# A new written order for the first five groups of an attention and two-layer kernel, with the first transposes in PSUM banks of their own

## The chip, the cores and the metric

The kernel runs on one core of a Trainium2 chip. The metric is the device time of one execution in microseconds (us), the median over repeated runs. Engines are named as the profile names them: PE (TensorE matmul) and PEld (its weight loads), DVE (VectorE), ACT (ScalarE), POOL (GpSimd), SP (SyncE, which here only issues transfers).

## The reference

```python
# attention: 4 sequences, 8 heads, 768 positions, 64 per head
scores = scale * q @ k.T                       # per sequence and head
keep   = (pos_k < 8) | ((0 <= rel) & (rel < 96))   # 8 global keys, 96 local ones
dist   = where(global and not local, 96, abs(rel))
scores = where(keep, scores - slope[h] * dist, -1e9)
a      = softmax(scores);  attn = a @ v
# two layers on the 3072 tokens of 512
x = attn.transpose(0, 2, 1, 3).reshape(3072, 512)
h = x @ w_in                                   # 512 -> 2048
g = max(h, 0) + log1p(exp(-abs(h)))            # softplus
out = g @ w_out                                # 2048 -> 512, float32
```

## The kernel before

The 3072 tokens are 24 blocks of 128. Two neighbouring blocks of one sequence are a unit (12 of them), and two blocks are a group of 256 tokens for the two layers (12 groups). A block needs the keys of itself, of the block before it, and the 8 global keys of its sequence, which are copied over unused rows of the block before.

Every piece of work is an operation with a name, made by `op(name, engine, ...)`. The string `ORDER` lists all 1046 names in one sequence, each with the engine that runs it (P = PE, V = DVE, A = ACT, G = POOL, S = SP); the program is issued in exactly that sequence, so each engine has its own fixed queue, in the order of the string. An engine that waits holds up all that is behind it in its queue. The names:

- `ldq3`, `ldk3`, `ldv3` load unit 3; `win0` to `win7` and `wout0` to `wout7` load the 512 KB pieces of the weights, all through SP (the first q also through ACT). `castq`, `castk`, `castv`, `cin`, `cout` turn them into bf16.
- `trq`, `trk` transpose q and k: for units 0 to 2 on PE, into PSUM, with `cpq`, `cpk` copying them out; from unit 3 on by DMA transposes that SP issues.
- `sb` writes the bias into PSUM by a matmul (blocks 0 and 1), `sc6.0` are the scores of block 6 (two parts for some blocks), `z` adds the bias on DVE, `ex` is the exponential on ACT, `pv` the product with v, `nm` the normalisation on DVE, `xt`, `xc` the transpose of the block's result into XT (a DMA transpose from block 6 on). `gk`, `gv` copy global keys and values.
- `a5.3` is piece 3 of 8 of the first layer of group 5: 8 matmuls of 128x256 into one of two PSUM banks, h0 and h1 by turns; `e5.3` is its exponential on ACT, which frees the bank, and `ln5.1` the logarithm for two pieces.
- Groups 0 and 1 take the second layer plainly: `b0.1.4` are two matmuls of 128x512 of group 0, token block 1, from row piece 4 on; `oc` copies the sum out of PSUM. From group 2 on the 2x2 block product is made of seven products, `b2.3` and so on, of sums of weights (`ws`, made once) and of tokens (`ka`), with `oe` gathering them out of PSUM. `st` stores.
- `fill0` to `fill34` are matmuls on a blank tile that nothing reads. They write the bank x.

PSUM has eight banks: two tiles s0 and s1 of two banks each, h0, h1, x and o. Unit 0's transposes are made in two halves (`SPLIT`): both halves of q go to the two banks of tile s0 and both halves of k to those of s1. Accesses are ordered by a key for the whole tile (`held` cuts a key to its tile), so that the second half's score work waits for both halves' copies.

The operations that the prediction speaks of: the fillers (line 1235), unit 0's transposes (790) and their copies (793), later transposes on PE (810) and copies (817), score matmuls (950; block 0's are 887 and 897, block 1's bias is 931), first-layer matmuls (1060), plain second-layer matmuls (1107), weight casts (643), casts of q, k, v (658, 674, 686, 706), first-layer exponentials (1075).

## Time and profile before

| what | value |
|---|---|
| median of 3 runs | 210.25 us (210.16 to 210.38) |
| span of the profiled execution, first to last instruction | 208.3 us |
| mean granted TensorE clock | 0.997 |
| busy in the span | PE 97%, ACT 81%, DVE 77%, POOL 54% |
| moved by DMA | 40.99 MB, mean 197 GB/s |

The profiled execution's span leaves out what lies ahead of its first and behind its last instruction, so it is 1.95 us below the median of the runs. Rows of the profile give start and length, engine, line, operation, output<-input; `x8` is the number of instructions that a row merges. `[0.66 <-ACT ident_q]` is idle time in front of it and what ended it. The end of a matmul is modelled, and neighbouring matmuls overlap in such rows. Times are from the span's start.

### The profile page before, as it was taken

The page shows a single profiled execution, that of the slowest core. Times are in us where ns is not written, and L with a number is a line of the kernel's source. Part 1 is how long each engine was busy: PE and PEld are TensorE (multiplying, and loading weights), DVE is VectorE, ACT ScalarE, POOL GpSimd, SP SyncE. Part 2 cuts the span into 40 slices and gives each one's busy share as a digit, 9 for nine tenths or more (in the row PEclk, how much of TensorE's full clock was granted, in tenths as well). Part 3 has the DMA queues.
Part 4 walks back from the last instruction along what each step waited for, and adds up shares of the span by engine and source line. Part 5 has one row for each costly group of instructions (what it writes and reads, how often), then busy time and mean ns, then how long its engine had stood idle before and what let it go on. Part 6 is the DMA issues. An engine that isn't in the chain of part 4 may idle for free.

```text
span 208.3 us, 5515 instructions
## 1 busy us (share of the span) xinstructions
PE 201.5 (97%) x2211; PEld 164.8 (79%) x2211; DVE 159.8 (77%) x296; ACT 169.0 (81%) x240; POOL 112.8 (54%) x127
## 2 busy tenths in 40 slices
PE   7789999999999999999999999999999999999993
PEld 2455887756678889888888898888888889888882
DVE  5589899899888798786989995928897684434383
ACT  4698899998999987998879989679879895897300
POOL 4356262708686367742867699655707506623540
PEclk9999999999999999999999999999999999999998
DMA  5999999999998999679999979573742204200205
GB/s 175 364 361 388 387 358 361 332 245 249 201 271 214 257 210 312 172 188 296 195 212 259 191 200 221 145 152 102 106 73 62 92 5 142 63 0 0 104 22 181
DMA packets 70650, 40.99 MB, mean 197 GB/s; under 512 B 30433, under 2 KB 62689, under 8 KB 70625
## 3 DMA queue, kind: packets, MB, share of 16 engines
q1 hardware_dynamic: 69936, 39.99, 77.2%
q10 hardware_dynamic: 688, 0.66, 1.0%
q8 instruction: 17, 0.28, 0.5%
q14 instruction: 9, 0.07, 0.1%
HBM read 27.26 MB, written 6.29 MB: 161 GB/s over the span
## 4 chain that ended last, share of the span: by engine, by line
PE 85%; DMA 8%; DVE 2%; POOL 2%; issue 1%; ACTq 0%; ACT 0%; POOLq 0%; DVEq 0%
PE h_ps L1060 38%; PE o_ps L521 25%; PE s_ps L950 5%; PE x_ps L1002 4%; PE s_ps L1107 3%; DMA raw<-in_q_dram 3%; DMA kT<-kb 3%; DMA XT<-xs 2%; PE x_ps L1235 2%; PE x_ps L521 2%; PE s_ps L521 1%; PE s_ps L810 1%; POOL vb L706 1%; PE o_ps L1107 1%; PE o_ps L1002 1%
## 5 line engine op out<-in xcount | busy, mean ns | idle before, releaser
L1060 PE MATMUL h_ps<-XT,w_in_bf 128*128 128x256 bf16 x768 | 94.4, 273 | 0.1
L1060 PEld LDWEIGHTS <-w_in_bf 128*128 128x128 bf16 x768 | 73.2, 98 | 11.0 <-DMA XT<-xs 0.3
L1075 ACT ACTIVATE e<-h_ps 128x512 f32<-128x512 f32 x96 | 60.1, 637 | 17.6 <-PE h_ps L1060 16.6
L1086 ACT ACTIVATE g<-e 128x1024 bf16<-128x1024 f32 x48 | 49.8, 1053 | 0.6
L976 DVE TENSOR_TENSOR z<-s_ps,biasA 128x1024 f32<-128x1024 f32 x38 | 45.9, 1218 | 3.5 <-PE s_ps L950 3.1
L983 ACT ACTIVATE pb<-z 128x1024 bf16<-128x1024 f32 (+1 forms) x44 | 43.4, 993 | 1.3 <-DVE z L976 0.6
L451 POOL TENSOR_TENSOR g<-g 128x1024 bf16<-128x1024 bf16 x11 | 23.9, 2171 | 23.7 <-DVE raw L451 23.5
L521 PEld LDWEIGHTS <-g 128*128 128x128 bf16 x320 | 30.9, 98 | 3.6
L451 POOL TENSOR_TENSOR raw<-g 128x1024 bf16<-128x1024 bf16 x9 | 19.6, 2177 | 15.0 <-ACT g L1086 13.5
L868 POOL COPY vb<-vb 4x512 bf16<-4x512 bf16 x22 | 14.9, 675 | 20.9 <-PE x_ps L1002 16.2
L706 POOL CAST vb<-raw 64x512 bf16<-64x512 f32 x32 | 21.6, 678 | 6.0 <-DMA raw<-in_v_dram 4.7
L521 PEld LDWEIGHTS <-raw 128*128 128x128 bf16 x240 | 22.6, 98 | 2.8
L521 PE MATMUL o_ps<-raw,raw 128*128 128x256 bf16 x192 | 24.3, 273 | 0.0
L451 DVE TENSOR_TENSOR raw<-g 128x1024 bf16<-128x1024 bf16 x21 | 17.2, 829 | 6.5 <-ACT g L1086 4.1
L521 PE MATMUL o_ps<-raw,g 128*128 128x256 bf16 x160 | 19.6, 273 | 0.0
L1002 PEld LDWEIGHTS <-pb 128*128 128x128 bf16 x352 | 16.4, 98 | 3.6 <-ACT pb L983 0.6
L1014 DVE TENSOR_TENSOR xs<-x_ps,rcp 128x256 bf16<-128x256 f32 x40 | 17.0, 424 | 1.4
L1002 PE MATMUL x_ps<-vb,pb 128*128 128x65 bf16 x304 | 15.8, 193 | 0.0
L521 PE MATMUL o_ps<-w_out_bf,g 128*128 128x256 bf16 x128 | 15.8, 273 | 0.0
L1235 PE MATMUL x_ps<-blank 128*128 128x512 bf16 x35 | 11.7, 454 | 1.2 <-DVE blank L1159 1.2
L1013 DVE RECIPROCAL rcp<-x_ps 128x4 f32<-128x4 f32 x40 | 7.1, 178 | 7.4 <-PE x_ps L1002 6.8
L674 POOL CAST qb<-raw 128x1024 bf16<-128x1024 f32 (+1 forms) x9 | 9.3, 1032 | 5.9 <-DMA raw<-in_q_dram 5.6
(123 smaller groups left out, 216.3 us busy)
## 6 DMA issues: line engine op xcount, KB each, us to landing
raw<-in_v_dram SPq DMA_DIRECT2D x12, 512.0 KB, 5.7
out_dram<-osb SPq DMA_DIRECT2D x22, 256.0 KB, 2.5
raw<-in_q_dram SPq DMA_DIRECT2D x9, 512.0 KB, 4.9
raw<-in_k_dram SPq DMA_DIRECT2D x9, 512.0 KB, 5.5
raw<-in_moe_w_in_dram SPq DMA_DIRECT2D x8, 512.0 KB, 9.3
raw<-in_moe_w_out_dram SPq DMA_DIRECT2D x8, 512.0 KB, 9.1
raw<-in_k_dram SPq DMA_DIRECT2D x6, 256.0 KB, 5.9
raw<-in_q_dram SPq DMA_DIRECT2D x4, 256.0 KB, 7.0
```

Of the source, the lines that this page charges most:

```text
L451: (nc.vector if eng == "DVE" else nc.gpsimd).tensor_tensor(dst, a[0], b[0], ALU.subtract)
L521: nc.tensor.matmul(psum(j), lhs[:, f // 2, f % 2, :], w(f), start=(f == 0 and not (chain and j in "267")), stop=(f == 7), skip_group_check ...
L706: copy_on[eng](dst, src)
L868: copy_on[eng](vb_of(prev)[sl, :, 0:D], vb_of(first)[sl, :, 0:D])
L976: nc.vector.tensor_tensor(z, src, bias, ALU.add)
L983: nc.scalar.activation(pb[:, 0:nr, :].rearrange("p (y a) b -> p y (a b)", y=2), src, AF.Exp, scale=1.0 / root_d)
L1002: nc.tensor.matmul(xv[:, h, :], pb[:, 4 * (h % 2) + 2 * part + h // 2 if lone else u_all * (2 * (h % 2) + h // 2) + u, :], vb_of(prev if u ...
L1014: nc.vector.tensor_tensor(xs[:, 4 * part : 4 * part + 4, :], xv[:, :, 0:D], rcp[:][:, :, None].to_broadcast([P, 4, D]), ALU.mult,)
L1060: last = nc.tensor.matmul(hv[:, j, :], w_in_bf[:, m, fb * P : fb * P + P], XT[g % NXG][:, m, :], start=(m == 0), stop=(m == NM - 1),)
L1075: nc.scalar.activation(e[:, p % 2, :, :].rearrange("p j (b t r) -> p (j b) r t", b=2, r=2), hb[:].rearrange("p (a r t) -> p a r t", a=4, r=2),
L1086: nc.scalar.activation(gt[:, 2 * p - 2 : 2 * p + 2, :].rearrange("p a t -> p (a t)"), e[:].rearrange("p a j t -> p (a j t)"), AF.Ln, bias=1.0,
L1235: nc.tensor.matmul(x_ps[:], blank[:, 0:P], blank[:])
```

## The change

Four things change.

1. `ORDER` is written anew from the start to the fourth group's second-layer products on PE (`b3.4` is the first of a tail of 154 PE operations that is the same in both; the other engines' tails agree from about the same place). The set of operations is the same. 76 of them run on another engine.
2. Unit 0's transposes get a home each (`SPLIT_KEYS`): q's halves go to the first bank of s0 and to o, k's halves to the first bank of s1 and to x, and each is ordered by its own bank.
3. The fillers are made in two lots: 22 ahead of all loads, the others behind unit 0, ordered against all users of the bank x, since a transpose of k is now made there.
4. The copies of global keys and values are no longer held behind the exponential of the block before; what they read and write still orders them.

In `ORDER`, 19 fillers stand ahead of the first transposes `trq0.0` (12 before) and 16 behind it (23 before). On SP the first 27 transfers are the same; behind `wout5` the order changes up to the transfers of unit 7. On PE the scores of block 4 and the first half of block 5 (`sc4.0`, `sc5.0`) now stand ahead of the first-layer piece `a0.7`; before, `sc5.0` stood behind `b0.0.4`. A piece of the string, where `sc5.0` is now, and the rest of the diff:

```diff
-nm3.1:V cin6:G a0.4:P e0.5:A cpq2.0:V wout4:S xt3:P e0.4:A cin7:V sc4.0:P xc3:V ln0.2:A a0.7:P wout5:S z4.0:V cout0:G
+cin5:V pv3.0:P ex3.1:A sc4.0:P nm3.0:V cin4:G e0.3:A z4.1:V pv3.1:P fill34:P gk5:A a0.5:P e0.2:A cin6:G z4.0:V wout4:S
...
-FILLERS = 35
+FILLERS = 22, 35
...
+SPLIT_KEYS = {"q": (("s", 0, 0), ("o",)), "k": (("s", 1, 0), ("x",))}
...
         if i in SPLIT:
             for x in range(2):
-                tr = s_ps[key[1]][:, x, :].bitcast(BF16)[:, 0:512]
+                home = SPLIT_KEYS[which][x]
+                tr = bank(home).bitcast(BF16)[:, 0:512]
...
-                sub = [("sub", which, i)] if x else []
                 op(f"tr{which}{i}.{x}", "PE", 0.225, rank + 0.05 * x, mm, count=4,
-                   reads=[(which + "b", i % NQB, 2 * x + z) for z in range(2)] + ["ident_q"] + (held([key]) if x else []),
-                   writes=sub or held([key]))
+                   reads=[(which + "b", i % NQB, 2 * x + z) for z in range(2)] + ["ident_q"], writes=held([home]))
                 outs = [("qT", i % NQT, x)] if which == "q" else [kt_tile(i) + (x, r) for r in range(2)]
-                op(f"cp{which}{i}.{x}", engs[x % len(engs)], 0.0, rank + 0.1 * x, ev, reads=held([key]) + sub,
+                op(f"cp{which}{i}.{x}", engs[x % len(engs)], 0.0, rank + 0.1 * x, ev, reads=held([home]),
                    writes=outs, alts={"DVE": 0.36, "ACT": 0.51})
...
         op(f"gk{n}", "POOL", 0.25, rank, copies,
-           reads=kt_keys(first), writes=kt_keys(prev), after=since, port=True,
+           reads=kt_keys(first), writes=kt_keys(prev), port=True,
            alts={"POOL": 0.25, "DVE": 0.14, "ACT": 0.14})
...
-    def filler(j):
-
+    def fillers(js):
         def fn():
             nc.tensor.matmul(x_ps[:], blank[:, 0:P], blank[:])
-        return op(f"fill{j}", "PE", 0.216, 1e6 + j, fn, reads=["blank"],
-                  after=[pl.writer[("x",)]] if j else [])
+        for j in js:
+            last = op(f"fill{j}", "PE", 0.216, 1e6 + j, fn, reads=["blank"], after=users(("x",)))
+            pl.writer[("x",)], pl.readers[("x",)] = last, []
...
-    for j in range(FILLERS):
-        pl.writer[("x",)] = filler(j)
+    fillers(range(FILLERS[0]))
...
             attend_in(i, at_block(n0) - 6.0)
+            if not i:
+                fillers(range(*FILLERS))
```

Three places as the engines' queues show them. The first is POOL's queue where the later pieces of w_in are cast, before (cin2, castq2.0, gk8, gv8.1, cin6, and the casts of w_out):

```order
L643 CAST w_in_bf<-raw_76 128x2x512
L674 CAST qb_81<-raw_69 128x8x64
L852 COPY kTa_92<-kTa_92 128x4x8
L868 COPY vb<-vb 4x8x64
L643 CAST w_in_bf<-raw_67 128x2x512
L643 CAST w_out_bf<-raw_72 128x1024
```

and now (cin2, castq2.0, castk2.1, cin4, cin6, cin7, gk8, cout0):

```order
L644 CAST w_in_bf<-raw_76 128x2x512
L675 CAST qb_81<-raw_69 128x8x64
L675 CAST kb_83<-raw_68 128x8x64
L644 CAST w_in_bf<-raw_77 128x2x512
L644 CAST w_in_bf<-raw_67 128x2x512
L644 CAST w_in_bf<-raw_79 128x2x512
L852 COPY kTa_92<-kTa_92 128x4x8
L644 CAST w_out_bf<-raw_72 128x1024
```

Two pieces of w_in, raw_77 (cin4) and raw_79 (cin7), have come from DVE to POOL, and one half of k's cast with them.

The second is ACT's queue from the exponential e1.2 to the copies of group 0's output, before:

```order
L1075 ACTIVATE e_106<-h_ps_64 128x4x2x64
L1075 ACTIVATE e_106<-h_ps_65 128x4x2x64
L643 CAST w_out_bf<-raw_75 128x1024
L1086 ACTIVATE g_107<-e_104 128x1024
L1075 ACTIVATE e_104<-h_ps_65 128x4x2x64
L643 CAST w_out_bf<-raw_77 128x1024
L674 CAST qb_82<-raw_67 128x1024
L1075 ACTIVATE e_104<-h_ps_64 128x4x2x64
L1086 ACTIVATE g_108<-e_106 128x1024
L1038 COPY XT_120<-x_ps 128x4x128
```

and now:

```order
L644 CAST w_out_bf<-raw_75 128x1024
L1075 ACTIVATE e_106<-h_ps_64 128x4x2x64
L707 CAST vb<-raw_74 64x8x64
L1075 ACTIVATE e_106<-h_ps_65 128x4x2x64
L1086 ACTIVATE g_107<-e_104 128x1024
L1086 ACTIVATE g_108<-e_105 128x1024
...
L1086 ACTIVATE g_108<-e_106 128x1024
L1075 ACTIVATE e_104<-h_ps_65 128x4x2x64
L1075 ACTIVATE e_104<-h_ps_64 128x4x2x64
...
L687 CAST kb_84<-raw_68 128x1024
L983 ACTIVATE pb_100<-z_95 128x1024
```

The casts of v of unit 2 (raw_74, three of them) and of k of unit 3 (raw_68) have come to ACT; one cast of w_out (raw_77), the cast of q of unit 3 (raw_67) and the copy to XT have left it.

The third is SP's queue from the loads of unit 3 on, before:

```order
L608 DMA raw_67<-in_q_dram 128x8x128
L608 DMA raw_68<-in_k_dram 128x8x128
L639 DMA raw_79<-in_moe_w_out_dram 128x2x512
L639 DMA raw_78<-in_moe_w_out_dram 128x2x512
L608 DMA raw_69<-in_v_dram 128x8x128
L837 DMA_TRANSPOSE qT_85<-qb_82 128x8x128
L608 DMA raw_74<-in_q_dram 128x8x128
L830 DMA_TRANSPOSE kT_89<-kb_84 128x8x64
L608 DMA raw_75<-in_k_dram 128x8x128
```

and now:

```order
L640 DMA raw_78<-in_moe_w_out_dram 128x2x512
L609 DMA raw_69<-in_v_dram 128x8x128
L609 DMA raw_68<-in_k_dram 128x8x128
L609 DMA raw_67<-in_q_dram 128x8x128
L640 DMA raw_79<-in_moe_w_out_dram 128x2x512
L609 DMA raw_74<-in_q_dram 128x8x128
L830 DMA_TRANSPOSE kT_89<-kb_84 128x8x64
L837 DMA_TRANSPOSE qT_85<-qb_82 128x8x128
```

wout7 (raw_79) has moved behind v, k and q of unit 3, the load of q of unit 4 (raw_74) ahead of unit 3's transposes, and k's first transpose ahead of q's.

167 lines of the change are left out of this document (83 added, 84 removed).

## The prediction

> **What bounds the kernel now.** I read the page first, then busy times by stretch, then the filler matmuls, then the chain of waits. The page's first part and its slices:
>
> ```profile
> PE 201.5 (97%) x2211; PEld 164.8 (79%) x2211; DVE 159.8 (77%) x296; ACT 169.0 (81%) x240; POOL 112.8 (54%) x127
> PE   7789999999999999999999999999999999999993
> DMA  5999999999998999679999979573742204200205
> ```
>
> TensorE is busy from the third slice to the last; the DMA engines are full for the first dozen slices (5.2 us each). By stretches (length, then PE, PEld, DVE, ACT, POOL, and the granted clock, DMA share, GB/s):
>
> ```profile
> 6.70:16.00 9.30, 8.08 (x108) 5.25 (x107) 6.57 (x19) 7.94 (x14) 5.03 (x8) 1.00 1.08 366
> 16.00:28.40 12.40, 12.40 (x153) 9.39 (x147) 10.71 (x25) 10.85 (x17) 5.81 (x8) 1.00 1.05 387
> 28.40:50.00 21.60, 21.60 (x202) 14.66 (x199) 20.74 (x35) 20.69 (x28) 9.86 (x13) 1.00 1.14 308
> 50.00:66.00 16.00, 15.79 (x190) 11.82 (x188) 14.28 (x25) 14.98 (x21) 11.14 (x17) 1.00 1.17 220
> 66.00:90.00 24.00, 24.00 (x280) 20.96 (x277) 20.40 (x36) 21.32 (x30) 15.81 (x20) 1.00 1.05 235
> 90.00:200.00 110.00, 110.00 (x1241) 97.04 (x1240) 78.21 (x134) 89.62 (x124) 62.38 (x54) 1.00 0.59 132
> ```
>
> TensorE is idle for 1.22 us (9.30 - 8.08) between 6.7 and 16, and from there on only for 0.21 us between 50 and 66. Part of what it does is filler, though. The filler line alone, over the whole run and by stretch, and three rows of the timeline:
>
> ```profile
> L1235 PE MATMUL x_ps<-blank x35: 378/379/634, 1.2 to 25.6; 128*128 128x512 bf16 x35
> 6.70:12.50 5.80, 1.57 (x5) 0.40 (x5) 1.00 1.10 352
> 12.50:28.40 15.90, 5.22 (x18) 1.59 (x18) 1.00 1.05 387
> 28.40:208.00 179.60, 0.00 (x0) 0.00 (x0) 1.00 0.76 174
> 1.17 4.90 PE L1235 MATMUL x_ps<-blank 128*128 128x512 bf16 x12 [1.17 <-DVE blank L1159]
> 6.72 0.38 PE L790 MATMUL s_ps<-ident_q,qb 128*128 128x128 bf16 x4 [0.66 <-ACT ident_q L1170]
> 19.72 1.24 PE L1235 MATMUL x_ps<-blank 128*128 128x512 bf16 x5
> ```
>
> Five fillers take 1.24 us where one alone shows 0.38, so each occupies (1.24 - 0.38) / 4 = 0.216 us and a lone matmul shows some 0.16 us of tail that the next one overlaps. So TensorE's time is: 6.72 us before the first useful matmul, useful work that no order changes, 23 fillers of 0.216 = 4.97 us after that, and waits. From 28.4 us to the end no filler is left and hardly a wait: what the change does beyond there can only be lost, or gained in tenths. What the changed order can win lies ahead of 28.4 us, and all that counts is how much useful work TensorE has behind it there.
>
> **The early orders.** After the change 19 fillers stand ahead of the first transposes, not 12. Eleven of the twelve old ones start by 5.69 us (1.17 + 4.90 = 6.07 us is the end of the twelfth, less its 0.38 us); seven more and that twelfth put trq0.0 at 5.69 + 8 x 0.216 = 7.42 us, 0.70 us later than 6.72. Its inputs are earlier, so the fillers decide. Behind it 16 fillers stand where 23 stood: 7 x 0.216 = 1.51 us less. If no wait changed, the gain would be 1.51 - 0.70 = 0.81 us; the waits decide.
>
> The first loads keep their order, so they keep their arrival; these rows start when one lands:
>
> ```profile
> 5.65 0.62 ACT L658 CAST qb<-raw 128x512 bf16<-128x512 f32 x1 [0.45 <-DMA raw<-in_q_dram]
> 6.41 0.43 DVE L658 CAST kb<-raw 128x512 bf16<-128x512 f32 x1 [0.29 <-DMA raw<-in_k_dram]
> 7.32 0.61 POOL L658 CAST qb<-raw 128x512 bf16<-128x512 f32 x1 [2.42 <-DMA raw<-in_q_dram]
> 7.90 0.87 DVE L658 CAST kb<-raw 128x512 bf16<-128x512 f32 x1 [0.87 <-DMA raw<-in_k_dram]
> 10.53 1.09 ACT L910 ACTIVATE pb<-h_ps 128x512 bf16<-128x512 f32 x2 [0.77 <-PE h_ps L897]
> 15.75 0.41 PE L950 MATMUL s_ps<-qT,kTa 64*128 64x128 bf16 x8 [0.48 <-ACT kTa L817]
> ```
>
> The second q half is cast on VectorE (0.43 us, as the k row shows) from 7.3 to 7.75 and the second k half on GpSimd (0.61) from 7.9 to 8.5; if VectorE took 0.87 again, trq0.1 would still be ready at its turn. Transposes in banks of their own then follow each other without waiting for one another's evacuation: trq0.0 7.42, trk0.0 7.85, trq0.1 8.28, the bias seed 8.7, and block 0's scores at 9.2 us. The ScalarE row above, the first exponential, would start near 9.6 instead of 10.53. From there softmax, normalisation and the transposes of unit 1 chain through ScalarE and VectorE much as before, and sc2.0 comes at about 15.6 us against 15.75: the lead is spent again. Three rows of weights set the posts after that:
>
> ```profile
> 19.98 1.04 POOL L643 CAST w_in_bf<-raw 128x1024 bf16<-128x1024 f32 x1 [1.57 <-DMA raw<-in_moe_w_in_dram]
> 26.52 1.04 POOL L643 CAST w_in_bf<-raw 128x1024 bf16<-128x1024 f32 x1
> 27.39 0.71 DVE L643 CAST w_in_bf<-raw 128x1024 bf16<-128x1024 f32 x1 [0.37 <-DMA raw<-in_moe_w_in_dram]
> 28.43 1.92 PE L1060 MATMUL h_ps<-XT,w_in_bf 128*128 128x256 bf16 x16
> 17.71 0.40 PE L950 MATMUL s_ps<-qT,kTa 64*128 64x128 bf16 x8
> 18.05 0.39 PE L1235 MATMUL x_ps<-blank 128*128 128x512 bf16 x1
> ```
>
> The changed order wants a0.2 next after the first pieces, and its w_in piece (cin2) is cast at 19.98 + 1.04 = 21.02 us: a0.2 waits about 0.5 us for it. The last post is cin7: it lands at 27.39 as now, but its cast moves from VectorE (0.71) to GpSimd (1.04), so a0.7 can start at about 27.39 + 1.04 = 28.43, which is where it starts now. What has been done by then differs: sc4.0 runs three microseconds earlier, and half of block 5's scores, sc5.0, is already done. Eight score matmuls cost 18.05 - 17.71 = 0.34 us and another 0.1 us in front, where they follow wider matmuls. So **term one: -0.43 us**, from a post that the DMA sets. Below it the end is TensorE's own pace: with cin7 in time it would be there some 0.2 us sooner. Above it is zero, should a0.7 come 0.4 us late.
>
> **From 28.4 to 50 us.** Here TensorE, ScalarE (20.69 of 21.60) and VectorE (20.74) are all full, and the change gives ScalarE more work. Prices per piece, ScalarE between 28 and 48 us by groups, and two rows of the timeline, the second being sc6.0:
>
> ```profile
> L1075 ACT ACTIVATE e<-h_ps 128x512 f32<-128x512 f32 x11 | 7.0, 644 | 0.5 <-PE h_ps L1060 0.4
> L643 ACT CAST w_out_bf<-raw 128x1024 bf16<-128x1024 f32 x2 | 2.1, 1044 | 0.0
> L1136 ACT COPY osb<-s_ps 128x512 f32<-128x512 f32 x1 | 0.6, 586 | 0.5 <-PE s_ps L1107 0.5
> L852 ACT COPY kT<-kTa 128x32 bf16<-128x32 bf16 x1 | 0.2, 237 | 0.0
> 49.48 0.62 ACT L706 CAST vb<-raw 64x512 bf16<-64x512 f32 x1
> 49.06 0.62 PE L950 MATMUL s_ps<-qT,kT 64*128 64x128 bf16 x16
> ```
>
> To ScalarE come, between the first exponential and sc6.0: two w_in casts (1.04 each; the trace has only w_out's on ScalarE, the same size, and two casts of 0.62 would be 1.24), three v casts and two casts of q and k (0.62 each), one cast of a whole k (1.04), cpq2.0 and oc0.1.0 (0.59 each) and a short copy (0.24): 7.6 us. Away go two casts of 1.04, xc1, xc4, cpk2.1 and cpq1.1 (0.59 each), one v cast (0.62) and two short copies (0.48): 5.5 us. Net +2.1 us. Against that stand the earlier start (0.9) and ScalarE's idle time, 1.55 us in 16 to 28.4 (12.40 - 10.85) and 0.91 in the next stretch, 2.46 together. If all of it is used, ScalarE ends this stage 1.3 us earlier than now; if none is, 1.2 us later. I take it as just keeping up, since it idles for z tiles and matmuls that come earlier in the new order. Walking the rows, b0.1.14 falls near 46.6, oc0.0.0 ends near 48.5 and sc6.0 starts near 48.6, while now it starts at 49.06: the 0.43 of term one, kept. **Term two: 0**, between -0.5 (TensorE's own pace, if it got there sooner) and +1.6 (1.2 late, and term one lost).
>
> The transfers here: k of the fourth unit before q, and wout7 behind both. The queue is full, so wout7 comes two loads later (2 x 0.52 MB at 308 GB/s, 3.4 us); walking the queue, its cast ends near 46.3 against b0.1.14's turn at 46.6, and the transposes of the fourth unit land near 48.3 against sc6.0 at 48.6. Cover is 0.3 us for each; where it is gone, the stall is as long as the lateness.
>
> **From 50 us.** The 0.21 us of idle time are three pauses, and each hides a 0.16 us overlap as well: about 0.6 us in all. Rows of the timeline for the first and the chain of waits for the others:
>
> ```profile
> 52.41 0.42 PE L1002 MATMUL x_ps<-vb,pb 128*128 128x65 bf16 x8
> 52.39 5.58 DMA kT<-kb
> 58.02 0.62 PE s_ps L950 x16
> 60.56 4.29 DMA XT<-xs
> 64.90 1.92 PE h_ps L1060 x16
> ```
>
> At 52.41 pv6.0 waits for its exponential; the new order puts a third first-layer piece (0.87 us) in front of it. At 58.02 the scores of block 8 wait for the DMA transpose of k; the new order issues it ahead of ldv4 and ldq5, two loads of 1.7 us each at that rate, and the wait was 0.3 us. At 64.90 a3.1 waits for the transposed block 7, which queues behind trq5 now and ahead of it then. All three go: -0.6. I give 0.15 back for b1.1.0, whose bank is freed by oc1.0.0, moved from ScalarE to a full VectorE. **Term three: -0.45** (0 to -0.6). Beyond, both orders keep TensorE full, and from b3.4 on they are the same, so what is gained by then stays. Weight sums and token sums that move to GpSimd are the dearest pieces there:
>
> ```profile
> L451 POOL TENSOR_TENSOR g<-g 128x1024 bf16<-128x1024 bf16 x11 | 23.9, 2171 | 23.7 <-DVE raw L451 23.5
> ```
>
> Even at 2.17 us, ka2.2, the last of them before convergence that TensorE takes soon, ends a microsecond before b2.2 by my walk; if it did not, b2.2 would wait for what is missing.
>
> **Sum.** -0.43 + 0 - 0.45 = -0.88 us on a span of 208.3 us, 207.4. The runs stand at 210.25, 1.95 above the span; the same distance gives **209.4 us**.
>
> **The rivals.** *More is won*: the early chain keeps its lead of 0.9 us, the new waits are none. The most it can be: now 4.97 of fillers and some 2.5 of waits (1.22 with four overlaps of 0.16, and 0.6), then 0.70 + 16 x 0.216 = 4.16 and no wait: 3.3 us, 207.0. Against it: the weights' arrivals do not move. From 208.6 down to half of that, 0.14. *It cancels*: cin7 or a late evacuation eats term one and the DMA queue shifts its own stall; 209.83 to 210.67, chance 0.22. *Slower, by ScalarE*: its added work is not absorbed between 20 and 48 us, the banks of first-layer pieces come free late, and TensorE waits for e tiles between a1.1 and sc6.0. It decides from the point where ScalarE recovers less than 1.2 us (2.1 - 0.9) of its 2.46 us of idle time; with none, sc6.0 is 1.2 us late, less the 0.45 of term three: +0.75, 211.0. For it: ScalarE is at 96% (20.69 of 21.60) there, and three v casts stand in the middle of its new list. Against it: nine pieces leave it in the same stage. Chance 0.14. *Slower, by the clock*: seven fillers fewer let TensorE pause, and its clock drops. The twelve fillers of the 4.90 us row stand (4.90 - 0.38) / 11 = 0.41 us apart, not 0.216; such a spell again costs 11 x 0.19 = 2.1 us: 211.5. The longest pause in the trace after the start is 0.66 us and the clock column stays at 1.00; my longest new wait is 0.55. Chance 0.03. The Trainium skill's page "TensorE: Matmul & The Clock Gate", section "What's actually happening", has the clock halve after an idle window of about 3.4 us; by that rule nothing drops here, and the trace agrees, 0.66 us of pause with a clock of 1.00. *The orders don't do what they say* has no room: they are the program's own instruction order.
>
> **How the numbers follow.** The forecast, 208.6 to 209.83, has 0.47, more gained 0.14, cancelled 0.22, slower 0.17. A difference of 0.2%, 0.42 us, is about the least that a measurement of this kernel tells from none: faster 0.61, same 0.22, slower 0.17. The range is 208.3 to 210.9: it leaves out the larger part of the big gain and of the slow cases. The likeliest case's own range is 208.6 to 209.8.
>
> **What would show it.** Right: trq0.0 near 7.4; the first exponential near 9.6; a0.7 near 28.4 with sc5.0 ahead of it; sc6.0 near 48.6; no TensorE idle time at the places of 52.41, 58.02 and 64.90. Wrong: idle time of TensorE in front of first-layer pieces, released by ScalarE, between 30 and 48 us; sc6.0 released by a DMA; b0.1.14 behind the cast of wout7; a first-layer piece behind a w_in cast later than 28.9.

## The result, and the profile after

The changed kernel took 212.87 us (median; single values 212.19, 212.23, 213.51, 213.52) against 210.31 us of the kernel before beside it: ratio 1.0113, 95% interval 1.0078 to 1.0148. It is slower by 1.1%; the forecast was 209.4 us. Measured again on another chip it took 214.77 us (212.90 to 215.44) against 210.56: ratio 1.0179 (1.0142 to 1.0216). The profiled execution took 212.23 us with a span of 210.4 us, 2.1 us more than the 208.3 before; what follows looks at that execution first, and then at others.

The page of the changed kernel, its first part and two rows of its slices (forty equal slices of the span, the granted clock and the DMA engines' busy share in tenths):

```profile
PE 202.2 (96%) x2202; PEld 163.9 (78%) x2211; DVE 161.6 (77%) x300; ACT 171.8 (82%) x245; POOL 110.4 (52%) x118
PEclk9999999999999999999999999999999999999999
DMA  5999999998999999999999969675651302300205
```

Nine matmul records are missing (2202 of 2211), so idle time of TensorE is better read from starts than from busy sums. Its granted clock is full throughout. The waits of TensorE in that page's execution (who waited for what, sum, times, longest); none of the three reached 0.2 us in the kernel before:

```profile
PE h_ps L1060 <- DMA XT<-xs: 1.3, 2, 0.7
PE s_ps L950 <- DMA kT<-kb: 0.4, 1, 0.4
PE s_ps L950 <- DMA qT<-qb: 0.2, 1, 0.2
```

Four rows of the timeline of the changed kernel, TensorE, are its posts: a0.7 (merged with no other), sc6.0, sc13.0, and the last row of products; behind them the last two of these in the kernel before:

```profile
28.27 0.60 PE L1060 MATMUL h_ps<-XT,w_in_bf 128*128 128x256 bf16 x4
49.02 0.56 PE L950 MATMUL s_ps<-qT,kT 64*128 64x128 bf16 x14
91.30 0.40 PE L950 MATMUL s_ps<-qT,kTa 64*128 64x128 bf16 x8
206.25 0.82 PE L522 MATMUL h_ps<-raw,raw 128*128 128x256 bf16 x6
```

```profile
90.05 0.45 PE L950 MATMUL s_ps<-qT,kTa 64*128 64x128 bf16 x10
203.68 0.71 PE L521 MATMUL h_ps<-raw,raw 128*128 128x256 bf16 x5
```

The matmuls that stand ahead of sc6.0 are the same set in both orders, and so are those ahead of sc13.0; from sc13.0 on the sequence is the same too. So the differences of these starts are gains and losses, without any correction:

| start of | before | changed | difference |
|---|---|---|---|
| a0.7 (with sc5.0, 0.43 us, done only in the changed one) | 28.43 | 28.27 | -0.16, with sc5.0 -0.59 |
| sc6.0 | 49.06 | 49.02 | -0.04 |
| sc13.0 | 90.05 | 91.30 | +1.25 |
| last row of products | 203.68 | 206.25 | +2.57 |
| end of the span | 208.3 | 210.4 | +2.1 |

The early order won 0.59 us by 28 us and had lost it by 49. From sc6.0 to sc13.0 it lost 1.29 us, and 1.32 us more behind sc13.0, where both kernels run the same matmuls in the same sequence. (What lies behind the last products was 0.44 us shorter; nothing here was tried on that.) The places, in TensorE's timeline of the changed kernel (pv7.0, a3.1, sc10.0, sc14.0, a6.0; idle time in brackets):

```profile
58.75 0.40 PE L1002 MATMUL x_ps<-vb,pb 128*128 128x65 bf16 x8
65.76 0.50 PE L1060 MATMUL h_ps<-XT,w_in_bf 128*128 128x256 bf16 x3 [0.61 <-DMA XT<-xs]
73.33 0.57 PE L950 MATMUL s_ps<-qT,kT 64*128 64x128 bf16 x14 [0.17 <-DMA qT<-qb]
96.93 0.23 PE L950 MATMUL s_ps<-qT,kT 64*128 64x128 bf16 x2 [0.41 <-DMA kT<-kb]
109.45 0.61 PE L1060 MATMUL h_ps<-XT,w_in_bf 128*128 128x256 bf16 x4 [0.67 <-DMA XT<-xs]
```

Each idle time in brackets hides an overlap besides, because rows that follow each other without a wait overlap (a first-layer piece starts 0.16 us before the shown end of the row ahead, a score piece 0.07). With it the waits are: a3.1 0.78, sc10.0 0.24, sc14.0 0.48, a6.0 0.84. There are smaller ones at pv7.0 (0.30), at pv7.1 (0.28, for the normalisation nm7.0), at sc11.0 (0.15) and at sc8.0 (0.10). Together that is 3.2 us, where the kernel before has 0.5 at pv6.0, sc8.0 and a3.1. Up to sc13.0 the waits add up to 1.8 us against 0.5 before, and behind it to 1.3 against none: that is the whole of the two losses, +1.29 and +1.32.

Which transpose comes late is not the same in every execution. A second profiled execution of the same kernel (after_again below) waits 0.84 us at pv8.0, 0.83 at sc11.0, 0.60 at sc7.0 and 0.55 at a6.0, but 0.07 at a3.1 and not at all at sc14.0; from sc6.0 to its last products it takes 157.48 us against 157.23 here. So the sum hardly varies and the places do, and a single wait below 1 us in one trace is weak evidence for what an edit does.

**How a3.1 came to wait in this execution.** The chain of waits of the changed kernel from 58 to 66 us:

```profile
58.20 0.64 DVE vb L868
58.84 1.13 DVE z L976
60.09 0.42 DVE xs L1014
60.52 0.59 DVE kT L855 x2
61.23 0.42 DVE xs L1014
61.68 4.04 DMA XT<-xs
65.76 0.28 PE h_ps L1060
```

The transposed block 7 (xt7) is issued at 61.68 instead of 60.56, and takes 4.04 us. In front of it VectorE has no gap: two copies of global values (57.06 to 58.84), the bias sum z8.0, and only then the normalisations nm7.0 and nm7.1. In the kernel before nm7.0 stood ahead of z8.0 and one of the copies was on GpSimd. GpSimd meanwhile shows why pv7.0 was late (timeline, changed kernel: castk5.0, ws3.7, castv3.11):

```profile
55.74 1.04 POOL L687 CAST kb<-raw 128x1024 bf16<-128x1024 f32 x1 [1.26 <-ACT g L1086]
56.74 1.28 POOL L417 TENSOR_TENSOR raw<-raw 128x512 bf16<-128x512 f32 x1
58.08 0.61 POOL L707 CAST vb<-raw 64x512 bf16<-64x512 f32 x1
```

castv3.11 needs v of unit 3, there since 40.43, but stands behind a cast that waits for ldk5 (landed 55.59, whatever the row names) and behind a weight sum.

**How sc14.0 and a6.0 came to wait.** sc14.0 needs the transpose trk7.0, which in the new order of SyncE stands behind xt11, a store and the load ldq8, and stood ahead of all three before. Its row in SyncE's queue (issue time, how long SyncE was held), changed and before:

```profile
92.34 1.39 SPq L830 DMA_TRANSPOSE kT<-kb  x1
```

```profile
85.15 2.01 SPq L830 DMA_TRANSPOSE kT<-kb  x1
```

In the changed kernel it landed at 96.88, and sc14.0 started at 96.93. So SyncE's two orders agree only from the load ldv9 on (93.79 in the changed kernel) and GpSimd's only from castk8.0 on, later than TensorE's, which agree from b3.4. The place of trk7.0 was not changed by itself in any run; in gv7_on_gpsimd below it has the same place, landed at 95.68, and sc14.0 did not wait.

The next three transposes in SyncE's queue, changed and before (trk7.1, xt12, xt13):

```profile
97.04 3.91 SPq L830 DMA_TRANSPOSE kT<-kb  x1
101.05 1.21 SPq L1045 DMA_TRANSPOSE XT<-xs  x1
105.08 1.22 SPq L1045 DMA_TRANSPOSE XT<-xs  x1
```

```profile
94.35 3.36 SPq L830 DMA_TRANSPOSE kT<-kb  x1
97.81 1.37 SPq L1045 DMA_TRANSPOSE XT<-xs  x1
102.51 1.19 SPq L1045 DMA_TRANSPOSE XT<-xs  x1
```

SyncE runs 2.6 to 3.2 us behind, while TensorE at sc13.0 is 1.25 us behind: the queue is later than the work that waits for it. For xt13, the transpose that a6.0 waits for, this can be followed. Its input is ready at 104.22 us against 102.48 before, 1.74 later, as much as TensorE itself is late by then. Before, SyncE issued it at once; in the changed kernel SyncE is busy with trk8.0 and a store until 104.98. That costs 0.83 us more, which is the wait of a6.0. The stretches of the changed kernel that answer to those of before (length, then busy time of PE, PEld, DVE, ACT and POOL with the number of instructions, granted clock, DMA share, GB/s):

```profile
28.40:50.00 21.60, 21.35 (x190) 14.22 (x191) 20.17 (x37) 20.12 (x29) 9.52 (x11) 1.00 1.03 294
50.00:66.00 16.00, 14.95 (x178) 10.63 (x180) 15.53 (x25) 15.14 (x20) 11.01 (x13) 1.00 1.07 205
66.00:90.00 24.00, 23.75 (x278) 20.71 (x275) 19.61 (x38) 21.10 (x32) 11.11 (x11) 1.00 1.11 228
90.00:200.00 110.00, 108.91 (x1229) 95.56 (x1227) 78.69 (x134) 91.48 (x127) 61.51 (x55) 1.00 0.65 138
```

Length times rate: from 28.4 to 90 us 21.6 x 14 + 16 x 15 + 24 x 7 = 710 KB less were moved than before, 3.1 us at 228 GB/s, and they are made up for behind 90 us (110 x 6 = 660 KB).

### The profile page after: what moved, and what is told of

The parts are those of the page before. It is cut to its first block, busy times and chain, and to the rows that moved or that the text cites. A ratio compares the mean times of both kernels' runs of the same rounds, so it can differ in the third digit from the quotient of the medians.

```text
span 210.4 us, 5489 instructions
## 1 busy us (share of the span) xinstructions
PE 202.2 (96%) x2202; PEld 163.9 (78%) x2211; DVE 161.6 (77%) x300; ACT 171.8 (82%) x245; POOL 110.4 (52%) x118
## 2 busy tenths in 40 slices
DMA packets 70648, 40.98 MB, mean 195 GB/s; under 512 B 30432, under 2 KB 62688, under 8 KB 70624
## 4 chain that ended last, share of the span: by engine, by line
PE 70%; DVE 11%; DMA 9%; ACT 6%; issue 2%; SPq 0%; DVEq 0%
PE h_ps L1060 29%; PE o_ps L522 21%; DMA kT<-kb 5%; PE x_ps L1234 4%; DMA XT<-xs 4%; DVE z L976 4%; PE s_ps L950 4%; PE x_ps L1002 4%; PE s_ps L1107 3%; ACT pb L983 2%; ACT e L1075 2%; DVE xs L1014 2%; PE x_ps L522 2%; PE s_ps L522 1%; PE o_ps L1107 1%
## 5 line engine op out<-in xcount | busy, mean ns | idle before, releaser
L1075 ACT ACTIVATE e<-h_ps 128x512 f32<-128x512 f32 x96 | 59.3, 633 | 16.4 <-PE h_ps L1060 16.0
L452 POOL TENSOR_TENSOR g<-g 128x1024 bf16<-128x1024 bf16 x13 | 28.1, 2167 | 30.7 <-DVE raw L452 28.9
L452 POOL TENSOR_TENSOR raw<-g 128x1024 bf16<-128x1024 bf16 x7 | 15.3, 2193 | 15.2 <-ACT g L1086 13.7
L452 DVE TENSOR_TENSOR raw<-g 128x1024 bf16<-128x1024 bf16 x23 | 18.2, 798 | 5.8 <-ACT g L1086 3.5
L707 POOL CAST vb<-raw 64x512 bf16<-64x512 f32 x26 | 16.6, 642 | 3.3 <-DMA raw<-in_v_dram 2.1
L868 POOL COPY vb<-vb 4x512 bf16<-4x512 bf16 x17 | 11.6, 681 | 9.1 <-ACT qT L817 6.7
L1234 PE MATMUL x_ps<-blank 128*128 128x512 bf16 x33 | 11.2, 456 | 1.5 <-DVE blank L1159 1.2
L687 POOL CAST kb<-raw 128x1024 bf16<-128x1024 f32 x6 | 6.2, 1039 | 11.8 <-DMA raw<-in_k_dram 10.5
```

Of the source, the lines that this page charges most:

```text
L452: (nc.vector if eng == "DVE" else nc.gpsimd).tensor_tensor(dst, a[0], b[0], ALU.subtract)
L707: copy_on[eng](dst, src)
L868: copy_on[eng](vb_of(prev)[sl, :, 0:D], vb_of(first)[sl, :, 0:D])
L1075: nc.scalar.activation(e[:, p % 2, :, :].rearrange("p j (b t r) -> p (j b) r t", b=2, r=2), hb[:].rearrange("p (a r t) -> p a r t", a=4, r=2),
L1234: nc.tensor.matmul(x_ps[:], blank[:, 0:P], blank[:])
```

## The experiments

All kernels below have the same matmuls ahead of sc6.0 and ahead of sc13.0, so their profiled executions can be set side by side by the same posts (after_12fill and merge31_12fill have seven fillers fewer at the start). The posts of a row are those of one profiled execution, which can lie some us from the median: first49_new's took 216.54 us, first28_old's 217.75, gv7_and_sp2's 213.70, and after_again's 212.90, its quickest. Times are medians beside the kernel before on the same chip (its own medians: 210.3 to 210.6). In the diffs `-` is what the kernel they start from has, one queue per line.

| kernel | sc6.0 | sc6.0 to sc13.0 | sc13.0 to last products | time, us | ratio (95%) |
|---|---|---|---|---|---|
| before | 49.06 | 40.98 | 113.63 | | |
| changed | 49.02 | 42.28 | 114.95 | 212.87 | 1.0113 (1.0078-1.0148) |
| first28_new | 50.21 | 40.65 | 113.63 | 211.38 | 1.0051 (1.0025-1.0077) |
| first49_new | 51.16 | 45.70 | 113.63 | 214.33 | 1.0146 (1.0086-1.0206) |
| first28_old | 53.40 | 43.42 | 114.95 | 215.75 | 1.0258 (1.0196-1.0320) |
| first49_old | 48.89 | 43.63 | 115.12 | 214.65 | 1.0184 (1.0143-1.0224) |
| v_cast_first | 49.33 | 43.08 | 115.12 | 213.07 | 1.0115 (1.0079-1.0152) |
| gv7_on_gpsimd | 49.38 | 41.49 | 114.97 | 211.98 | 1.0079 (1.0049-1.0108) |
| sp_old_from_xt7 | 49.27 | 46.01 | 114.11 | 215.95 | 1.0264 (1.0217-1.0311) |
| gv7_and_sp | 49.30 | 49.78 | 114.87 | 219.82 | 1.0424 (1.0386-1.0462) |
| gv7_and_sp2 | 50.68 | 42.36 | 114.60 | 211.93 | 1.0086 (1.0056-1.0116) |
| after_no_stores | 50.80 | 41.88 | 114.19 | 212.86 | 1.0107 (1.0070-1.0145) |
| after_again | 49.43 | 43.27 | 114.21 | 214.77 | 1.0179 (1.0142-1.0216) |
| after_12fill | 49.35 | 43.28 | 114.45 | 212.63 | 1.0104 (1.0065-1.0143) |
| merge31 | 48.51 | 42.06 | 113.63 | 210.84 | 1.0015 (0.9995-1.0034) |
| before_trk4 | 49.34 | 41.92 | 113.72 | 210.84 | 1.0019 (1.0003-1.0035) |
| merge31_trk4 | 49.06 | 41.64 | 113.63 | 210.89 | 1.0012 (0.9996-1.0027) |
| merge31_12fill | 48.78 | 41.38 | 113.63 | 210.63 | 0.9997 (0.9978-1.0016) |
| before_no_stores | 49.28 | 41.60 | 113.63 | 210.10 | 0.9982 (0.9964-1.0000) |
| merge31_no_stores | 50.16 | 41.10 | 113.63 | 210.86 | 1.0010 (0.9987-1.0033) |

**Which stretch loses.** Four kernels join the two orders at 28 or 49 us. At a seam the queues of the engines meet unprepared; the pieces show one queue of each (ACT, SP, PE, PE; `|` is the seam).

```diff
 first28_new, ACT
-e0.5 ex4.0 e0.4 ln0.1 e0.7 e0.6 ex5.0 e1.1
+e0.5 ex4.0 | ln0.1 e0.4 ln0.2 e0.7 e0.6 e1.1
 first49_new, SP
-trk3.1 ldk5 trq4 trk4.0 ldv4 ldq5
+trk3.1 ldk5 | ldv4 trq4 ldq5 trk4.0
 first28_old, PE (before)
-xt3 sc4.0 a0.7 a0.6 b0.0.0
+xt3 sc4.0 | sc5.0 a0.7 sc5.1 a0.6 b0.0.0
 first49_old, PE (before)
-xt5 sc6.0 b1.0.12 b1.0.14 a2.1
+xt5 sc6.0 | a2.1 a2.0 b1.0.12 b1.0.14
```

> New order for all that the changed kernel starts before 28.2 us (up to the first-layer piece a0.7), the old order behind it on every engine; banks for the first transposes as changed. Theory (the early part pays 0.6 to 0.7 us, the loss comes later): 0.6 us below the kernel before, 209.7 against 210.3, with a0.7 near 28.3, sc5.0 ahead of it and no new idle time of TensorE behind it. Rival (the early order only moves the cost to later casts and loads): 210.3 or more.

> New order for all that the changed kernel starts before 49.0 us (up to the scores sc6.0), the old order behind it. Theory (0.5 us of new waits between 28 and 49: for cout1, cout7 and the normalisation nm5.1; the large loss only behind 49): 0.1 us below the kernel before, 210.2. Rival (the loss is seeded before 49, by k, q and wout7 of the queue of transfers in another order): 211.5 to 212.3, as in the changed kernel.

> Old order for all that the kernel before starts before 28.4 us, the new order behind it. Theory (all that is lost is lost behind 28.4 us): 2.5 to 3.0 us above the kernel before, 213.0, slower than the changed kernel, since the early gain of 0.6 is missing. Rival (the early part causes the loss): 210.3.

> Old order for all that the kernel before starts before 49.0 us, the new order behind it. Theory (the loss behind 49 us is 2.0 to 2.4 us: pv7.0 waits for a v cast on GpSimd, then transposes by DMA wait in SyncE's queue): 212.5. Rival (those waits follow from what stands before 49): 210.3 to 210.8.

All four came out slower than expected, by waits at the seams: in first28_new e0.4 stands behind ln0.1 and a0.6 waits 1.07 us for it; in first28_old sc5.0 waits 2.5 us for z4.1; in first49_new trk4.0 stands behind ldk5, ldv4 and ldq5, and sc8.0 waits 2.2 us; in first49_old a2.1 waits 1.2 us for xc5. So their total times tell little about the stretches. One column does: behind sc13.0 the two of them with the old order from 49 us on take 113.63 us, the two with the new one 114.95 and 115.12. Over all kernels of the table it is 113.63 to 113.72 with the old order there and 114.11 to 115.12 with the new one. The loss there comes from what the new order does between 49 and 90 us, on other engines than TensorE. In first49_old the waits for DMA transposes add up too (TensorE's waits in that kernel):

```profile
PE s_ps L950 <- DMA kT<-kb: 2.0, 2, 1.4
PE h_ps L1060 <- DVE XT L1038: 1.2, 1, 1.2
PE s_ps L950 <- DMA qT<-qb: 0.6, 1, 0.6
```

**Block 7's lateness.** Two edits on the changed kernel's queues around 55 us:

```diff
 v_cast_first, POOL
-castk4.0 ws3.4 castk5.0 ws3.7 castv3.11 castv4.10
+castk4.0 ws3.4 castv3.11 castk5.0 ws3.7 castv4.10
 gv7_on_gpsimd, POOL and VectorE
-castk5.0 ws3.7 castv3.11 castv4.10
+castk5.0 castv3.11 gv7.1 ws3.7 castv4.10
-z7.1 nm6.1 gv7.1 gv8.0 z8.0 nm7.0
+z7.1 nm6.1 gv8.0 z8.0 nm7.0
```

> The changed kernel with one move: on GpSimd the last v cast of unit 3 (castv3.11) stands ahead of the k cast of unit 5 (castk5.0) and of a weight sum, where it stood behind both. Theory (what makes block 7 late is VectorE, full from 50 to 62 us; the normalisation nm7.0 stands behind the bias sum z8.0 there whatever pv7.0 does): pv7.0 no longer waits (0.31 us), pv7.1 waits as much longer, xt7 is issued at 61.7 as before the move, time unchanged within 0.3 us of the changed kernel. Rival (the late v cast is the cause): xt7 issued 0.3 to 1.1 us sooner, time 0.3 to 1.5 us below the changed kernel.

> The changed kernel with two moves on GpSimd: castv3.11 ahead of the weight sum ws3.7, and the copy of global values gv7.1 brought back from VectorE (1.11 us there) to GpSimd behind it. Theory (VectorE, full from 50 to 62 us, makes block 7's normalisation late, and with it the DMA transpose xt7 and SyncE's queue behind it): xt7 issued near 60.6 instead of 61.7, no wait in front of pv7.0 and a3.1 (1.1 us together), time 1.1 to 2.1 us below the changed kernel, 210.2 to 211.2 beside 210.3 of the kernel before. Rival (SyncE's order alone makes the transposes late): less than 0.4 us gained.

v_cast_first went as the theory said for its own place: pv7.0 no longer waits, xt7 is issued at 61.59, and the time is that of the changed kernel (213.07). In its profile pv8.0 waits 0.94 us for a v cast instead. gv7_on_gpsimd, which makes two moves at once, took the waits of pv7.0, a3.1, sc10.0 and sc14.0 away and is 0.8 us shorter than the changed kernel both from sc6.0 to the end (156.46 against 157.23) and in ratio (1.0079 against 1.0113 and 1.0115): the direction of the theory, less than its 1.1 to 2.1. The intervals of these ratios overlap, and xt7 was issued at 61.37 where 60.6 was expected. Its VectorE row, and what is left at a6.0:

```profile
59.15 0.18 DVE L1013 RECIPROCAL rcp<-x_ps 128x4 f32<-128x4 f32 x1
109.04 0.50 PE L1060 MATMUL h_ps<-XT,w_in_bf 128*128 128x256 bf16 x3 [1.17 <-DMA XT<-xs]
```

nm7.0 starts at 59.15 instead of 59.90, but pv7.1 is not in TensorE's turn before 60.26; the wait at a6.0 grew from 0.84 to 1.33 us. So in these two executions VectorE's full queue accounts for a3.1's wait and for some 0.8 of the 2.6 us, not for a6.0's. The times bear that out only weakly, and after_again shows that a3.1's wait can be absent without any edit.

**The order of SyncE's queue behind xt7**, three versions (of the changed kernel, and twice with gv7.1 moved):

```diff
 sp_old_from_xt7
-xt7 st1.0.0 st0.1.0 ldk6 trk5.0 ldv5 trq5 ldq6 xt8 ldq7 trk5.1 xt9 ldk7
+xt7 trq5 st0.1.0 ldv5 ldq6 trk5.0 ldk6 xt8 ldv6 trk5.1 xt9 ldq7 trq6
 gv7_and_sp
+xt7 trq5 ldk6 trk5.0 ldv5 st1.0.0 ldq6 xt8 st0.1.0 ldq7 trk5.1 xt9 ldv6
 gv7_and_sp2
+xt7 st0.1.0 trq5 ldk6 trk5.0 ldv5 ldq6 xt8 st1.0.0 ldq7 trk5.1 xt9 ldk7
```

> The changed kernel with SyncE's queue behind xt7 in the order of the kernel before (trq5 first, two output stores, ldk6 and ldv5 behind it, trk7.0 ahead of xt11 and ldq8); all other engines as changed. Theory (the waits of sc10.0, sc11.0, sc14.0 and a6.0 for DMA transposes, 1.7 us in all, come from transfers that stand ahead of them in the new queue): these four waits shrink to 0.5 us or less, time 1.2 us below the changed kernel. Rival (they are passed on from the late xt7, whatever the order behind it): no more than 0.3 us gained, a3.1 and a6.0 still wait.

> The kernel with gv7.1 back on GpSimd, and SyncE's queue behind xt7 rewritten so that it fits the new order of GpSimd: trq5 right behind xt7, the output stores of groups 0 and 1 later, ldv6 ahead of ldk7, trk7.0 ahead of xt11 and ldq8. Theory (the transposes of units 5 to 8 and block 13 are late because of what stands ahead of them in SyncE's queue): no wait for a DMA transpose over 0.4 us behind 66 us, where the kernel without this move shows 1.3 us in front of a6.0; time 1.0 to 1.5 us below it, 210.5 to 211.0 beside 210.4 of the kernel before. Rival (the transfers as a whole are behind, whatever their order): the wait moves to another transpose, less than 0.4 us gained.

> The kernel with gv7.1 back on GpSimd, and SyncE's queue behind xt7 with trq5 ahead of two loads, the output store of group 1's first block later, ldv6 and st1.1.0 in turn, and trk7.0 ahead of xt11 and ldq8; the store st0.1.0, which frees the buffer that oe2.a writes, stays early. Theory (order: the transposes are late for what stands ahead of them): the waits of a3.1, sc10.0, sc11.0, sc14.0 and a6.0 together under 0.8 us, where the kernel with gv7.1 alone shows 1.3 us in front of a6.0; 0.6 to 1.0 us below it. Rival (the transfers as a whole are behind): the sum of the waits stays within 0.4 us of that kernel's.

The first two failed by new waits and say nothing on the theory. In sp_old_from_xt7 ldk7 comes later, and GpSimd's new queue has its cast ahead of a copy that pv11.0 waits for, 2.50 us. In gv7_and_sp the store st0.1.0 was moved back by some 8 us, and oe2.a needs the buffer that it frees (VectorE's timeline):

```profile
76.79 0.69 DVE L483 COPY osb<-o_ps 128x512 f32<-128x512 f32 x1 [5.71 <-DMA out_dram<-osb]
```

gv7_and_sp2 keeps that store early. Behind sc13.0 it is 0.37 us shorter than gv7_on_gpsimd (114.60), in front of it 0.87 us longer (a3.1 waits 0.8 and sc8.0 0.7), the time the same (211.93 and 211.98); a6.0 still waits 0.7. That is the rival's case, the wait moves to another transpose; but this execution came to sc6.0 1.3 us later than gv7_on_gpsimd's, and sc8.0's transpose stands ahead of the place that was edited.

**Fewer transfers, and the early part alone.** merge31 takes the new order up to 31 us on the four engines and the old one behind it, with SyncE wholly old; it avoids the seams of the first four. The `_trk4` kernels bring trk4.0 forward; the `_no_stores` kernels leave out the four stores of groups 0 and 1.

```diff
 merge31, ACT, changed and merged
-ex4.0 e0.4 ln0.1 e0.7 e0.6 ex5.0 e1.1 e1.0 ln0.2
+ex4.0 e0.4 ln0.1 e0.7 e0.6 | ln0.2 e1.1 e1.0
 before_trk4 and merge31_trk4, SP and POOL, of the old order
-trq4 ldq5 trk4.0 ldk5 xt6 trk4.1 st0.0.0 trq5 xt7
+trq4 trk4.0 ldq5 ldk5 xt6 trk4.1 st0.0.0 xt7 trq5
-ws3.4 castq5.0 castv4.01 castv4.11 castv4.00
+ws3.4 castv4.01 castv4.11 castv4.00 castq5.0
 after_no_stores, before_no_stores, merge31_no_stores (from merge31_trk4)
+            if g >= FINE:
                 op(f"st{g}.{ns}.{a}", queue, 0.4, rank + 8.0 * c, st, dma=(0.72 * (z - a) / DM, 84.0), reads=keys)
```

> New order for all that the changed kernel starts before 31.0 us on TensorE, VectorE, ScalarE and GpSimd, so that the exponentials e0.4, e0.7 and e0.6 keep their new places; the old order behind it, SyncE's queue wholly in the old order, cout1 ahead of a copy of global values on GpSimd. Theory (the early part is worth 0.6 to 0.7 us and the rest of the old order has no loss in it): 0.4 to 0.7 us below the kernel before. Rival (what is won early is lost at the next post that the transfers set, the DMA transpose trk4.0 in front of sc8.0 or xt7 in front of a3.1): within 0.2 us of the kernel before, with that much more idle time of TensorE in front of sc8.0 or a3.1.

> The kernel before with three moves: on SyncE trk4.0 ahead of ldq5 and xt7 ahead of trq5, on GpSimd three v casts of unit 4 ahead of the q cast of unit 5. Theory (the transfers set the post of sc8.0, and TensorE waits there only 0.27 us in this kernel): 0.1 to 0.3 us below the kernel before. Rival (the transfers push each other and the wait comes back at a3.1 or sc10.0): the same time or up to 0.5 us more.

> The new order up to 31 us, the old one behind it, with the same three moves (trk4.0 ahead of ldq5, xt7 ahead of trq5, three v casts ahead of a q cast). Theory (the early part wins 0.7 to 0.9 us, which without these moves is lost as 1.23 us of waiting for trk4.0 in front of sc8.0): sc8.0 starts near 57.4 instead of 58.45, a3.1 near 64.5, time 0.6 to 1.0 us below the kernel before, 209.4 to 209.8. Rival (the transfers are at their limit up to 66 us, and a post that comes sooner makes another come later): 0.2 us or less below the kernel before.

> The changed kernel without the four output stores of groups 0 and 1 (256 KB each, 1 MB; 512 tokens are not written). Theory (from 56 to 110 us the transposes are late because transfers and SyncE's queue are full): the waits of sc10.0, sc11.0, sc14.0 and a6.0 (1.7 us) fall below 0.5 us; a3.1, whose transpose stands ahead of three of the stores, keeps at least 0.4 us of its 0.78; 1.2 us below the changed kernel. Rival (what is late is late by what it waits for on the engines): 0.3 us or less gained.

> The kernel before without the same four stores. It has only 0.16 us of waiting in front of a3.1 and none behind: no more than 0.2 us gained by every theory. It is the measure for the other two.

> The new order up to 31 us, the old one behind it with trk4.0 ahead of ldq5 and xt7 ahead of trq5, without the same four stores. Theory (the early part wins 0.6 to 0.7 us, which full transfers take back at a3.1, sc10.0 and sc11.0): those waits (1.0 us) vanish, and the time is 0.4 to 0.8 us below that of the kernel before without the stores. Rival (the early gain is no gain, the order of transfers has nothing to do with it): within 0.2 us of it.

merge31 is where the early gain went to be seen. It reaches sc6.0 0.55 us sooner than the kernel before, and then (chain of waits, trk4.0, sc8.0, xt7, a3.1):

```profile
52.31 6.10 DMA kT<-kb
58.45 0.62 PE s_ps L950 x16
61.00 4.38 DMA XT<-xs
65.43 0.61 PE h_ps L1060 x4
```

sc8.0 starts at 58.45 as against 58.02 before, after 1.06 us of idle time: the transpose was issued 0.08 us sooner than before and took 6.10 us instead of 5.58, so it did not land sooner. With trk4.0 ahead of ldq5 (merge31_trk4) that wait is gone, and sc10.0 waits 0.6 us instead; no time is won. before_trk4, the same three moves in the kernel before, is the rival's case too: sc8.0's wait is gone, and instead a3.1 waits 0.50 us, sc10.0 0.43 and sc11.0 0.36, at a ratio of 1.0019. The rivals of merge31 and merge31_trk4 put the idle time where it came and had no gain, as measured; by their medians the two kernels even lie 0.4 us above the kernel before, with intervals that include no difference. Set five kernels with the old order behind 31 us side by side (before, first28_new, merge31, merge31_trk4, merge31_12fill, the last two with the three moves): sc6.0 lies at 49.06, 50.21, 48.51, 49.06 and 48.78, yet sc13.0 at 90.05, 90.86, 90.57, 90.70 and 90.16. The two that are early at sc6.0 are not early at sc13.0.

Taking 1 MB of stores away did not settle why. From sc6.0 on after_no_stores is 1.2 us shorter than the changed kernel (156.07 against 157.23), as the theory said, with waits of 0.42 at a3.1 and none at sc10.0 and sc14.0. But 0.22 at sc11.0 and 0.57 at a6.0 are 0.8 us, more than the 0.5 that the theory allowed. Its early part was 1.8 us late in the profiled execution, so TensorE asked later, and the time did not move (212.86). The kernel before gained 0.5 us in its median where 0.2 at most was expected, but the interval reaches to no gain (0.9964 to 1.0000), and its trace has a wait of 0.95 us at sc8.0 where the kernel before has 0.18: when a transpose lands varies between executions here too. merge31_no_stores, which should have been 0.4 to 0.8 us below it, was 0.8 us above, so the theory that the early part is worth 0.6 us once transfers are lighter is not borne out. It is not settled either: in its profiled execution the early part was late (trq0.0 at 8.00 us, sc6.0 at 50.16), and from sc6.0 to the last products it took 154.73 us, 0.5 less than before_no_stores with the same stores left out.

**The start.** In the profiled execution of after_no_stores trq0.0 starts at 8.17 us, in that of the changed kernel at 7.37, with the same order. Two rows of their chains of waits, after_no_stores behind the changed kernel:

```profile
1.17 6.37 PE x_ps L1234 x19
```

```profile
1.17 7.17 PE x_ps L1235 x19
```

The same 19 fillers take 0.8 us longer, because they stand 0.43 us apart for longer before they change to 0.22. Over the traces of kernels with 19 fillers in front, trq0.0 starts anywhere from 6.68 to 8.17 us; with 12 in front, where its inputs decide, from 6.35 to 6.92. That alone does not make the early part late: executions in which trq0.0 starts between 6.35 and 7.83 us reach sc6.0 at 48.51 to 49.43 (first28_new, with its wait at the seam, at 50.21). Four others (first49_new, merge31_no_stores, gv7_and_sp2, after_no_stores), with trq0.0 at 7.71 to 8.17, reach it at 50.16 to 51.16. In exactly these four the small copy gk4 on VectorE takes 1.03 to 1.04 us beside a cast of w_in on GpSimd, and 0.16 to 0.17 in every other trace of the new early order (the rows stand in the last section). No run separates that copy from the rest, and there is no trace of the changed kernel's slower executions (213.5, 215 us), so it is not shown that this is what makes them slower.

after_12fill and merge31_12fill (on merge31_trk4) drop seven; after_again is the changed kernel once more:

```diff
-    fillers(range(FILLERS[0]))
+    fillers([j for j in range(FILLERS[0]) if not 12 <= j < 19])
```

> The changed kernel as it is, for more executions of it. Its four timings were two pairs, 212.2 and 213.5. Theory (the start of trq0.0 hangs on when the fillers ahead of it change from 0.43 to 0.22 us apart, which differs by up to 1.7 us between executions): values from 211.7 to 213.7, spread over the whole of it, spread of the kernel before under 1.5 us. Rival (the two pairs are chance): all within 0.5 us of one value.

> The changed kernel with seven fillers fewer ahead of the first transposes: fill12 to fill18 are gone, so that 12 stand ahead of trq0.0 as in the kernel before. Theory (19 fillers carry the uncertainty of their pace into trq0.0; 12 end before its inputs come in any case): trq0.0 near 6.5 us, spread of the times under 0.8 us, median 0.5 to 1.0 us below the changed kernel's. Rival (the fillers keep the matmuls' pace up, and without them the first ones run slow): no gain or a loss of up to 1 us.

> The new order up to 31 us with the old one behind it, trk4.0 ahead of ldq5 and xt7 ahead of trq5, and 12 fillers ahead of the first transposes. Theory (the early part is ahead by about 0.7 us in each execution, and the transfers take most of it back): 0.2 to 0.6 us below the kernel before. Rival (the posts that the transfers set up to 80 us leave nothing): within 0.2 us of the kernel before.

The second measurement of the changed kernel, 212.90 to 215.44 us, is spread widely as expected, but lies above the 211.7 to 213.7 that was given for it. On the same chip the seven fillers fewer took the median from 214.77 to 212.63 us, more than the 0.5 to 1.0 expected, and trq0.0 to 6.41; these are medians of six values each, and their ranges overlap. The spread did not go (211.81 to 214.34), so fillers are not its only source; the profiled executions of the two, both at the quick end of the fillers' range or without them, have the same length behind sc6.0 (157.5 and 157.7). merge31_12fill equals the kernel before (0.9997), as its rival said. No version that writes all of the output beat the kernel before.

## Why the prediction was wrong, step by step

- **Fillers and trq0.0**: 7.42 us forecast, 7.37 in the profiled execution; the step that the fillers decide was right, but "eleven of the twelve old ones start by 5.69" was taken from one execution, and that moment differs from one to the next. Twelve hid it behind the inputs' arrival; 19 put it in front of everything. The term was not a number but a range of 1.5 us, and the range I gave had no part for it. That 7.37 came so close to 7.42 was luck. The four executions above whose early part was late at sc6.0 all began late; how much of the changed kernel's median comes from this is not shown.
- **First exponential** 9.6: 9.66. **sc2.0** 15.6: 15.60. **a0.7** 28.43 with sc5.0 ahead: 28.27. **Term one**, -0.43: -0.59. Right in the main; the other 0.15 us came from the weight piece win7, which landed at 27.22 instead of 27.37 us.
- **Term two**, 0 between -0.5 and +1.6: +0.55. The posts were the ones named, cout7 and xt5, but the cover of 0.3 us was not there: b0.1.14 came at 46.86 right behind wout7's cast on VectorE (46.13 to 46.80), b0.0.2 at 35.03 behind cout1, which I had not walked at all, and xt5 behind a normalisation. These three waits are 0.20, 0.20 and 0.12 us, nearly the whole of the term. wout7 had landed at 45.20, 3.06 us later than before, about what was forecast; its cast began 0.9 us after that because three pieces stood ahead of it in VectorE's queue. So it was VectorE's queue and not the transfer, and the same holds for cout1 (wout1 landed at 29.90, its cast ran from 34.30 to 34.98). sc6.0 itself started without a wait. ScalarE, on which the largest rival rested, was no bound: 20.12 us busy of 21.60, and no first-layer piece waited for an e tile.
- **Term three**, -0.45, is the step that failed first: between sc6.0 and sc13.0 it was +1.29. "All three go": pv6.0's pause went, sc8.0's shrank to 0.1 us, a3.1's grew from 0.16 to 0.78, and pv7.0, pv7.1, sc10.0 and sc11.0 waited anew. I walked the place of xt7 in SyncE's queue, ahead of trq5, and not the time at which its input would be ready: four pieces had come to VectorE there (gv7.1, ws1.6, oc1.0.0, gk9; two had left it, gk7 and ws3.3) and nm7.0 had gone behind z8.0. In the one trace of gv7_on_gpsimd, with one of them moved back, that wait is gone. sc10.0 waits for trq5, the very transfer that was moved behind xt7 and five others (two stores, ldk6, trk5.0, ldv5).
- **"What is gained by then stays"**, from b3.4 on, is the step that failed worst: +1.32 with the same sequence on TensorE. The same order is the same time only if every queue that feeds it is the same too and arrives equally early. SyncE's was neither. Its orders differ until ldv9, with trk7.0 issued at 92.34 instead of 85.15, for which sc14.0 waits 0.48 us; and behind that it ran late, for which a6.0 waits 0.84 us. In after_again the same loss is divided otherwise, 2.29 us up to sc13.0 and 0.58 behind. All kernels with the new order between 49 and 90 us lose 0.5 to 1.5 us behind sc13.0, all with the old one less than 0.1.
- **Rivals**. "It cancels", with the DMA queue shifting its own stall, named the mechanism and priced it at no more than 0.2% of the time; it cost 2.6 us. The clock rival did not happen: the granted clock stayed at 1.00, no pause of the changed kernel was longer than 0.7 us.

What stays open: which of full DMA engines and SyncE's order makes the transposes late behind 66 us (two orders were tried without gain, and one lighter load with a gain only behind sc6.0), how much the place of trk7.0 alone costs, and why the changed kernel was slower still on the second chip, of which the trace shows only its quickest execution.

## What to carry to other kernels

Where the engines before a post are rearranged, walk the queue of transfers with the time at which each transfer's input is ready, not only with its place, and go on walking past the point from which the order is the same. Being early on the busiest engine is worth nothing if the next thing it needs is a transfer that does not come earlier. A run-up of variable length (filler matmuls) belongs behind a wait that covers it, not on the path.
